# Attention and gated MLP on one core: V of the first two batches by casting transfers, one k sum moved into the matmuls, norms in two parts

## The chip, the core and the metric

The kernel runs on one core of a Trainium2 chip. The core has a matrix engine (TensorE, PE in the profile), a vector engine (VectorE, DVE), a scalar engine for functions and copies (ScalarE, ACT), a general engine that also issues transfers (GpSimd, POOL) and an engine that only issues transfers (SyncE, SP). Each runs its own stream of instructions in order; semaphores join them. [...]

The metric is the device time of one execution in microseconds (us), the median of ten runs. A transfer issued from GpSimd can convert float32 to bf16 on the way (a casting transfer); one issued from SP moves bytes as they are.

## The reference

Inputs are q, k and v of shape (8 batches, 8 heads, 576 positions, 64), and two weight matrices of 512 x 2048 and 2048 x 512, all float32. The output is float32, 4608 x 512.

```python
q_d = q.reshape(B, H, Sd, 4, D).mean(axis=3)      # k_d, v_d likewise; Sd = 144
out_d = softmax_attention(q_d, k_d, v_d)
out_up = np.repeat(out_d, 4, axis=2)
mask = np.abs(pos[:, None] - pos[None, :]) < 4
out_local = softmax_attention(q, k, v, where=mask)
x = (out_up + out_local) as (4608, 512)
h = x @ w_in
out = (h * sigmoid(1.702 * h)) @ w_out
```

So each batch has two attentions, a banded one at full length (each query sees at most seven keys) and a full one at a quarter of the length, over sums of four neighbours. Their sum goes through two matrix layers.

## The kernel before

The order of the instructions is written out by hand (`tc.manual_schedule`), so the order in the source is the order on each engine. Waits between engines are set by the framework from what each instruction reads and writes; for PSUM it takes a whole tile's bank as one thing.

**Groups.** The 4608 rows are taken in nine groups of 512 (`TG`). The loop over `g` (line 896) does, for group g, layer 1 (`mm1`, 16 chunks `ffc` of four matmuls, then a SiLU on ScalarE) and layer 2 (`mm2`, 64 matmuls, then a copy and a store), and meanwhile prepares and computes the attention of batch g + 1. The steps of that attention are functions, put into the stream of `mm1` and `mm2` at numbered slots: slots 0 to 15 are before the chunks of `mm1`, slot 16 + n is before matmul n of `mm2`. `POS` (line 778) has the seven slots for groups 1 and on, `POS_0` those for group 0, `VDP_0` the slot of a step that only batch 1 has.

**Batch 0's attention stands before the loop** (lines 787 to 890). Here TensorE has nothing else to do, and `warm` puts in matmuls of zeros that nobody reads; one float32 `warm` shows as two matmul rows of 0.5 us. The start ends in `part`, which does layer 1 of group 0 for the first six chunks as the head pairs' `xT` come in.

**Steps of one batch.** Heads are taken in two quads (`qd`) for scores and in four pairs (`hp`) after that.

- `prep_1` (275): VectorE turns a loaded k or q tile (32 x 32 blocks) into `kT` or `qT`, with positions along the free axis and two bf16 values (`a`) per position.
- `pool_qk` (298): GpSimd adds four neighbouring positions to `kdT` and `qdT`, two instructions each. `pool_q_reduce` (289) does it for q in one instruction on VectorE.
- `scores` (373): 80 matmuls of 60 columns into two PSUM tiles of `PA`, for five stretches of 114 positions. In batch 0 `bar_others` first writes a large negative number outside the band (`barred`). `scores_d` (395): 24 matmuls of 144 columns into one tile, for the short attention.
- `exp_local`, `exp_down` (412, 419): ScalarE, to `es` and `eds`.
- `av_local0` and `av_down0` (517, 531; batch 0), `av` (430; others): the products with V, with a column of ones that gives the sum of each row. V is in `vbs` (bf16, five chunks of 128 positions) and its sums of four in `vds`, which `prep_vd_pe` (337) makes in batches 0 and 1 by matmuls with a 0/1 matrix and a ScalarE copy.
- `normalise0` (547; batch 0) and `normalise` (475): VectorE, a reciprocal of the row sums and one or two multiplications to y.
- `transp_sum` and `copy_x` (called by `turned`, 869; batch 0), `transp`, `copy_od` and `merge` (others): TensorE turns y back, the result goes to `xT`, the input of layer 1.

PSUM has three tiles `PA[0..2]` of two banks and two tiles `PM[0..1]` of one. `ps_tile` hands out `PA` in turn, counted in `turn["a"]`; in batch 0 head pairs 0 and 1 take `PA[0]` and `PA[1]`, head pair 2 takes `PA[2]` after that, head pair 3 `PA[0]` again.

**Transfers.** `load_qk` (211), `load_w_in`, `load_w_out` and `load_vb` (231) are issued on GpSimd and cast. `load_v` (215) and `load_v4` are issued on SP in float32. V of batch 0 comes by `load_v` (ten transfers) and is cast by VectorE, a chunk at a time (`prep_v`). V of batch 1 comes by `load_v` for chunks 0 to 2, cast by GpSimd, and by `load_vb` for chunks 3 and 4. Some transfers are held back by a one-element copy (a gate) into their target, which has to wait for something else: line 795 for V of batch 0, line 812 for the layer-1 weights, lines 905 and 907 in group 0.

Of the kernel before, what the change touches and what calls it, by code (L numbers as in the profile page):

```python
# [8 lines left out]
FP32 = mybir.dt.float32  # L9
# [10 lines left out]
def kernel(  # L20
# [16 lines left out]
    n_ffc = d_ff // 128  # L37
    n_groups = B * S // TG
    inv_sqrt_d = 1.0 / math.sqrt(D)
    KSTART = (0, 56)  # L40
    QSTART = (0, 60)

# [24 lines left out]

    PA = [psum.tile([128, 2, 512], FP32, name=f"pa{i}") for i in range(3)]
    PM = [psum.tile([128, 512], FP32, name=f"pm{i}") for i in range(2)]
    turn = {"a": 0, "m": 0}  # L70

    def ps_tile(n=None):
        if n is None:
# [200 lines left out]

    def prep_1(name, b, qd):
        store, dst = {"k": (kf, kT), "q": (qf, qT)}[name]
        tt = work.tile([128, S, 2], BF16, name=f"{name}T{qd}", tag=f"{name}T{qd}", bufs=1)
        t32 = tt.rearrange("p t a -> p (t a)").bitcast(FP32)
        nc.vector.transpose(  # L279
            out=t32.rearrange("p (i c) -> p c i", c=18),  # L280
            in_=store[b, qd].bitcast(FP32).rearrange("p (c d) -> p c d", c=18),
        )
        dst[b, qd] = tt
# [14 lines left out]
    def pool_qk(b, qd, names="kq"):  # L298
        for name, src in (("k", kT), ("q", qT)):
            if name not in names:  # L300
                continue
            sv = src[b, qd].rearrange("p (j f) a -> p j f a", f=4)
            t1 = work.tile([128, SD, 2, 2], FP32, name="pq", tag="pq")
            nc.gpsimd.tensor_tensor(  # L304
                out=t1, in0=sv[:, :, 0:2, :], in1=sv[:, :, 2:4, :], op=ALU.add
            )
            if name == "k":
                dst = kdT[qd][:, 0:SD, :]
            else:
                t = work.tile([128, SD, 2], BF16, name=f"qdT{qd}", tag=f"qdT{qd}", bufs=1)  # L310
                qdT[b, qd] = t
                dst = t
            nc.gpsimd.tensor_tensor(
                out=dst, in0=t1[:, :, 0, :], in1=t1[:, :, 1, :], op=ALU.add
            )
# [54 lines left out]
                skip_group_check=True,  # L370
            )

    def scores(b, qd, barred=False):
        sp = [ps_tile(), ps_tile()]
        if barred:
            bar_others(sp)
        for i in range(5):
            for a in range(2):
                for par in range(2):
                    for r in range(4):  # L380
                        rows = slice(32 * r, 32 * r + 32)
                        k0 = 114 * i + KSTART[par]
                        q0 = 114 * i + QSTART[par]
                        nc.tensor.matmul(  # L384
                            sp[r // 2][64 * par : 64 * par + 64, r % 2, 60 * i : 60 * i + 60],
                            lhsT=kT[b, qd][rows, k0 : k0 + 64, a],
                            rhs=qT[b, qd][rows, q0 : q0 + 60, a],
                            start=(a == 0 and not barred),
                            stop=(a == 1 or barred),
                            tile_position=(32 * r, 64 * par),  # L390
                            skip_group_check=barred,
                        )
        return sp

    def scores_d(b, qd, sd=None):
        sd = sd or ps_tile()
        bank = banks(sd)
        for kc in range(3):
            for a in range(2):
                for r in range(4):  # L400
                    rows = slice(32 * r, 32 * r + 32)
                    j = r % 2
                    nc.tensor.matmul(  # L403
                        bank[r // 2][64 * j : 64 * j + 64, SD * kc : SD * kc + SD],
                        lhsT=kdT[qd][rows, 48 * kc : 48 * kc + 64, a],
                        rhs=qdT[b, qd][rows, :, a],
                        start=(a == 0), stop=(a == 1),
                        tile_position=(32 * r, 64 * j),
                    )
        return sd  # L410

    def exp_local(qd, sp):
# [131 lines left out]
                    tile_position=(64 * j, 64 * pos),  # L544
                )

    def normalise0(o):
        yl = work.tile([128, 2, 6, D], BF16, name="yl", tag="yl", bufs=4)
        yd = work.tile([128, 2, 2, D], BF16, name="yd", tag="yd", bufs=4)
        rc = work.tile([128, 2, 7, 1], FP32, name="rc", tag="rc")  # L550
        ov = o[:, :, 0:455].rearrange("p x (c e) -> p x c e", e=65)
        nc.vector.reciprocal(rc, ov[:, :, :, 64:65])
        nc.vector.tensor_tensor(
            out=yd.rearrange("p s x d -> p x s d"), in0=ov[:, :, 4:7:2, 0:D],
            in1=rc[:, :, 4:7:2].to_broadcast([128, 2, 2, D]), op=ALU.mult,
        )
        nc.vector.tensor_tensor(  # L557
            out=yl, in0=ov[:, :, 0:6, 0:D],
            in1=rc[:, :, 0:6].to_broadcast([128, 2, 6, D]), op=ALU.mult,
        )  # L560
        return yl, yd

    def transp_sum(y, x):
        y, yd = y
        ups = [
            (0, 6, sub(x[0], 3, (1, 228)), sub(up, 3, (228, 2), (1, 114))),
            (0, 6, sub(x[0], 0, (1, 3)), sub(up, 0, (1, 3))),
# [85 lines left out]
    def attention(b, slots=None):  # L653
# [18 lines left out]

        def avn(*hps):
            def f():
                for n, hp in enumerate(hps):
                    st["o", hp] = av(b, hp, slots and slots[n])
                for hp in hps:
                    st["y", hp] = normalise(st["o", hp])
            return f

        def tr(*hps):
            def f():
                for n, hp in enumerate(hps):
                    st["x", hp] = transp(st["y", hp], slots and slots[n])
                for hp in hps:
                    od = copy_od(st["x", hp])
                    merge(b, hp, st["x", hp], od)
            return f

        return [lambda: s_pe(0), lambda: s_act(0), s1, avn(0, 1), avn(2, 3), tr(0, 1), tr(2, 3)]  # L690

    def hps_mm(g, ffc, dmc, acc):
        nc.tensor.matmul(  # L693
# [82 lines left out]
            f()  # L776

    POS = [13, 16, 33, 42, 53, 62, 71]
    POS_0 = [16, 18, 27, 54, 68, 60, 76]
    VDP_0 = 52  # L780

    o, y, x = {}, {}, {}

# [8 lines left out]
    iota_psel()  # L792
    iota_up()
    fill()
    load_v(0, gate=after(kdT[1][0:1, SD, 0:1], nc.vector))
    warm(4)
    make_off()
    make_ident(di)
# [3 lines left out]
    make_up()  # L802
    prep_1("k", 0, 0)
    prep_1("q", 0, 0)
    pool_qk(0, 0)
    sp = scores(0, 0, barred=True)
    exp_local(0, sp)
    prep_1("k", 0, 1)
    prep_1("q", 0, 1)
    pool_q_reduce(0, 1)  # L810
    pool_qk(0, 1, "k")
    nc.gpsimd.tensor_copy(out=w_in_bf[0:1, 0, 0:1], in_=vf[0][0:1, 2, 0, 0:1])
    load_w_in(0, 512)
    load_w_in(512, 512)
    load_w_in(1024, 1024)
    for qd in range(NQ):
        load_qk(1, qd)
    load_w_out(0)
    load_w_out(1)
    for i in range(5):  # L820
        prep_v(0, nc.vector, i=slice(i, i + 1))
    warm(2)
    sd = scores_d(0, 0)
    exp_down(0, sd)
    sp = scores(0, 1, barred=True)
    exp_local(1, sp)
    for hp in range(2):
        o[hp] = PA[hp]
    warm(1)
    scores_d(0, 1, PM)  # L830
    for u in range(2):
        nc.scalar.activation(
            out=eds[1][:, u, 0:432], in_=PM[u][:, 0:432],
            func=AF.Exp, scale=inv_sqrt_d / 16.0,
        )
    nc.scalar.preload_act_table_set("silu_and_others")
    warm(1, t=PA[2][:, 0, :])
    for hp in range(2):
        av_local0(hp, o[hp], range(0, 3))
    warm(1, 384, PA[2][:, 0, :])  # L840
    for hp in range(2):
        av_local0(hp, o[hp], range(3, 4))
    prep_vd_pe(0, flat(PA[2]), range(0, 2))
    warm(1, 256)
    for hp in range(2):
        av_local0(hp, o[hp], range(4, 5))
    prep_vd_pe(0, pm_tile(), range(2, 3))
    warm(1, 256)
    for hp in range(2):
        av_down0(hp, o[hp])  # L850
        y[hp] = normalise0(o[hp])
    o[2] = PA[2]
    av_local0(2, PA[2], range(5))
    av_down0(2, PA[2])
    y[2] = normalise0(o[2])
    warm(1)
    warm(1, 256)
    make_mask()

    gT0 = new_gT()  # L860
# [11 lines left out]
        copy_x(0, hp, x)  # L872

    turned(0, None)
    o[3] = PA[0]
    av_local0(3, PA[0], range(5))
    av_down0(3, PA[0])
    y[3] = normalise0(PA[0])
    turned(1, 1)
    part((0, 1), 0)  # L880
    turned(2, 2)
# [7 lines left out]
    for ffc in range(6):  # L889
        silu(gT0, ffc, acc[ffc])  # L890

    def loads_2():
        load_v(2)
        load_v4(2)

    for g in range(n_groups):
        b = g + 1
        if g == 0:
            nc.gpsimd.memset(v4[32:64], 0.0)
            load_vb(1, 3)  # L900
            load_vb(1, 4)
            prep_qk(1, 0)
            pool_qk(1, 0)
            prep_qk(1, 1)
            load_v(1, gate=after(qf[1, 1][0:1, 0:1], nc.vector), chunks=range(3))
            pool_qk(1, 1)
            nc.gpsimd.tensor_copy(
                out=w_out_bf[0:1, 8, 0:1], in_=vf[1][0:1, 1, 0, 0:1]
            )
            load_w_out(2)  # L910
            load_w_out(3)
            for i in range(3):
                prep_v(1, nc.gpsimd, i=slice(i, i + 1))
            for qd in range(NQ):
                load_qk(2, qd)
            loads_2()
        elif b < B:
            if b > 2:
                load_v4(b)
# [50 lines left out]
```

## Time and profile before

| | |
|---|---|
| median of 10 runs | 329.1 us (327.51 to 333.52) |
| profiled execution, its own time | 329.75 us |
| its span, first to last instruction | 327.7 us |
| instructions in the span | 11050 |

Busy time of the engines by stage, from one table of windows (us; granted clock as a share of full speed; the DMA column is the mean busy share of the sixteen engines, over 1 where packets overlap):

| stage | PE | DVE | ACT | POOL | clock | DMA |
|---|---|---|---|---|---|---|
| 0 to 8.6: first loads, constants | 7.12 | 5.74 | 3.98 | 6.11 | 1.00 | 0.73 |
| 8.6 to 15.5: scores of batch 0 | 6.73 | 4.66 | 3.67 | 5.53 | 1.00 | 1.19 |
| 15.5 to 24.7: V products and norms of batch 0 | 9.14 | 5.06 | 4.63 | 7.44 | 1.00 | 1.15 |
| 24.7 to 40.4: layer 1 of group 0 | 15.23 | 7.59 | 10.29 | 10.01 | 1.00 | 1.30 |
| 40.4 to 66.1: layer 2 of group 0, attention of batch 1 | 21.30 | 12.43 | 12.99 | 5.84 | 1.00 | 1.08 |
| 66.1 to 327.7: the rest | 250.72 | 97.06 | 149.63 | 102.78 | 1.00 | 0.54 |

PE's busy time counts the fillers too, and a matmul's row is longer than the step to the next one: 128 x 512 bf16 matmuls have rows of 379 ns and follow each other every 216 ns.

In the views below, a row of a timeline has its start and length in us, the engine, the source line, the operation, the tiles it writes and reads, the shape, a count where equal rows are merged, and in brackets the idle time before it and what ended that.

### The profile page before, as it was taken

To read this page: it belongs to the slowest core of one execution; us is meant where nothing else is said; L and a number is where in the kernel's file an instruction comes from. 1 tells how busy PE (TensorE), PEld (TensorE's weight loads), DVE (VectorE), ACT (ScalarE), POOL (GpSimd) and SP (SyncE) were. 2 spreads that over 40 slices of the span, in tenths; PEclk is the share of its full clock that TensorE was granted. 3 is DMA by queue.
4 is the path that set the end of the run, shared out by engine and by line. 5 is a ranking of instruction groups with operands and counts; after the bars stand their busy time and mean duration, and the time that the engine had idled before them with its cause. 6 is when DMAs were issued, how large, how long until landed. Compare 5 with 4: busy or idle time off the path is not lost.

```text
span 327.7 us, 11050 instructions
## 1 busy us (share of the span) xinstructions
PE 310.2 (95%) x4908; PEld 159.0 (49%) x4962; DVE 132.5 (40%) x220; ACT 185.2 (57%) x322; POOL 137.7 (42%) x167
## 2 busy tenths in 40 slices
PE   8999979899999999999799999999999999999996
PEld 3564444445554555455444554455444544444444
DVE  6656342760676047703671277216730560000000
ACT  4645881566846582659166745775576646415611
POOL 7873861079406940596019901990098000000000
PEclk9999999999999999999999999999999999999999
DMA  7999999999817991699139942994180110011012
GB/s 123 185 196 210 183 134 196 191 234 222 151 68 156 206 155 36 159 198 191 39 103 181 191 110 72 198 191 126 50 160 3 66 38 32 0 68 62 0 54 75
DMA packets 63551, 41.08 MB, mean 125 GB/s; under 512 B 44048, under 2 KB 54416, under 8 KB 63504
## 3 DMA queue, kind: packets, MB, share of 16 engines
q1 hardware_dynamic: 52944, 26.42, 39.2%
q0 software_dynamic: 10416, 13.90, 24.9%
q8 instruction: 38, 0.62, 0.8%
q10 hardware_dynamic: 144, 0.07, 0.1%
q14 instruction: 9, 0.07, 0.1%
HBM read 44.83 MB, written 9.44 MB: 166 GB/s over the span
## 4 chain that ended last, share of the span: by engine, by line
PE 87%; DVE 5%; issue 4%; DMA 2%; ACT 1%; POOL 0%; ACTq 0%; DVEq 0%; POOLq 0%
PE pm L693 35%; PE pm L749 32%; PE pa L384 4%; PE pa L693 2%; PE pa L403 2%; PE pa L445 2%; DMA qb<-in_q_dram 2%; PE pa L467 2%; PE pa L749 2%; PE pa L498 2%; DVE xT L631 1%; PE pm L649 1%; PE pm L764 1%; DVE y L484 1%; DVE yl L557 1%
## 5 line engine op out<-in xcount | busy, mean ns | idle before, releaser
L693 PE MATMUL pm<-xT,w_in_bf 128*128 128x512 bf16 x528 | 120.3, 379 | 1.6 <-DVE xT L637 0.9
L749 PE MATMUL pm<-w_out_bf,gT 128*128 128x512 bf16 x493 | 114.1, 379 | 5.4 <-issue 5.2
L704 ACT ACTIVATE gT<-pm 128x512 bf16<-128x512 f32 x136 | 81.0, 598 | 46.1 <-PE pm L693 46.1
L693 PEld LDWEIGHTS <-w_in_bf 128*128 128x128 bf16 x576 | 55.6, 98 | 68.0 <-issue 1.9
L749 PEld LDWEIGHTS <-gT 128*128 128x128 bf16 x560 | 51.7, 98 | 59.5 <-issue 0.2
L304 POOL TENSOR_TENSOR pq<-kT 128x576 f32<-128x576 bf16 x16 | 18.5, 1158 | 98.1 <-DVE kT L279 98.1
L428 DVE TENSOR_TENSOR es<-es,mask 128x600 bf16<-128x600 bf16 x28 | 21.7, 791 | 90.8 <-ACT es L414 90.1
L734 ACT ACTIVATE osb<-pm 128x512 f32<-128x512 f32 (+2 forms) x35 | 20.8, 593 | 41.2 <-PE pm L749 37.3
L610 ACT COPY od<-pa 128x384 f32<-128x384 f32 (+1 forms) x56 | 18.4, 413 | 30.9 <-DVE y L484 18.7
L484 DVE TENSOR_TENSOR y<-pa,rc 128x896 bf16<-128x896 f32 x28 | 30.6, 1092 | 1.0
L631 DVE TENSOR_TENSOR xT<-pa,od 128x570 bf16<-128x570 f32 x28 | 21.1, 754 | 11.4 <-ACT od L610 11.0
L325 POOL TENSOR_TENSOR v<-v 112x512 f32<-112x512 f32 x18 | 22.8, 1265 | 0.0
L736 DVE TENSOR_SCALAR osb<-pm 128x128 f32<-128x128 f32 x1 | 0.3, 292 | 55.3 <-ACT osb L734 55.3
L414 ACT ACTIVATE es<-pa 128x600 bf16<-128x600 f32 x32 | 19.7, 668 | 2.8 <-PE pa L384 2.6
L279 DVE STREAM_TRANSPOSE kT<-kb 128x576 f32<-128x576 f32 x16 | 20.0, 1251 | 1.5 <-DMA kb<-in_k_dram 1.5
L279 DVE STREAM_TRANSPOSE qT<-qb 128x576 f32<-128x576 f32 x16 | 19.9, 1244 | 1.3 <-DMA qb<-in_q_dram 1.2
L304 POOL TENSOR_TENSOR pq<-qT 128x576 f32<-128x576 bf16 x15 | 17.2, 1146 | 0.0
L319 POOL CAST vb<-vf 128x2560 bf16<-128x2560 f32 (+1 forms) x9 | 16.1, 1809 | 0.0
L384 PEld LDWEIGHTS <-kT 32*64 32x64 bf16 x1280 | 12.0, 104 | 6.8 <-issue 5.6
L483 DVE RECIPROCAL rc<-pa 128x14 f32<-128x14 f32 x28 | 6.7, 241 | 20.7 <-PE pa L467 20.7
L420 ACT ACTIVATE ed<-pa 128x864 bf16<-128x864 f32 x15 | 13.5, 897 | 2.2 <-PE pa L403 2.2
L328 POOL TENSOR_TENSOR vd<-v 112x256 bf16<-112x256 f32 x18 | 13.7, 759 | 1.4
(104 smaller groups left out, 259.7 us busy)
## 6 DMA issues: line engine op xcount, KB each, us to landing
vf<-in_v_dram SPq DMA_DIRECT2D x76, 128.0 KB, 6.4
out_dram<-osb SPq DMA_DIRECT2D x35, 256.0 KB, 2.1
v<-in_v_dram SPq DMA_DIRECT2D x36, 192.0 KB, 5.8
kb<-in_k_dram POOLq DMA_DIRECT2D x16, 288.0 KB, 7.0
qb<-in_q_dram POOLq DMA_DIRECT2D x16, 288.0 KB, 9.3
w_out_bf<-in_moe_w_out_dram POOLq DMA_DIRECT2D x4, 512.0 KB, 8.3
w_in_bf<-in_moe_w_in_dram POOLq DMA_DIRECT2D x2, 512.0 KB, 8.5
w_in_bf<-in_moe_w_in_dram POOLq DMA_DIRECT2D x1, 1024.0 KB, 12.5
```

Of the source, the lines that this page charges most:

```text
L279: nc.vector.transpose(out=t32.rearrange("p (i c) -> p c i", c=18), in_=store[b, qd].bitcast(FP32).rearrange("p (c d) -> p c d", c=18),)
L304: nc.gpsimd.tensor_tensor(out=t1, in0=sv[:, :, 0:2, :], in1=sv[:, :, 2:4, :], op=ALU.add)
L325: eng.tensor_tensor(out=t1[0:112], in0=x[:, :, 0:2, :], in1=x[:, :, 2:4, :], op=ALU.add)
L384: nc.tensor.matmul(sp[r // 2][64 * par : 64 * par + 64, r % 2, 60 * i : 60 * i + 60], lhsT=kT[b, qd][rows, k0 : k0 + 64, a], rhs=qT[b, qd] ...
L414: nc.scalar.activation(out=es[2 * qd + u][:, :, 0:300], in_=sp[u][:, :, 0:300], func=AF.Exp, scale=inv_sqrt_d,)
L428: nc.vector.tensor_tensor(out=ev, in0=ev, in1=mask, op=ALU.mult)
L484: nc.vector.tensor_tensor(out=y[:, xs], in0=ov[:, :, :, 0:D], in1=rc[:, xs].to_broadcast([128, n, 7, D]), op=ALU.mult,)
L631: eng.tensor_tensor(out=sub(xT[hp], t0 + 3, (57, 2), (114, 5), (1, 57)), in0=sub(x, 3, (509, 2), (57, 5), (1, 57)), in1=sub(od, 3, (57, 2) ...
L693: nc.tensor.matmul(acc, lhsT=w_in_bf[:, dmc, ffc * 128 : (ffc + 1) * 128], rhs=xT[dmc][:, g * TG : g * TG + TG], start=(dmc == 0), stop=(d ...
L704: nc.scalar.activation(out=gT[:, ffc, :], in_=acc, func=AF.Silu, scale=GELU_SCALE)
L734: eng.activation(out=osb, in_=ap, func=AF.Copy, scale=1.0 / GELU_SCALE)
L749: nc.tensor.matmul(ops[t], lhsT=gT[:, ffc, t * 128 : (t + 1) * 128], rhs=w_out_bf[:, ffc, :], start=(ffc == 0), stop=(ffc == n_ffc - 1),)
```

## The change

V of batches 0 and 1 comes wholly by `load_vb`, ten casting transfers each, so the SP loads, the casts by VectorE and GpSimd and the four gates go. The loads of weights and of batch 1 move ahead of the constants' VectorE part in the source; on GpSimd they follow the ten V transfers at once. The sums of four of k for batch 0 are not made: `scores_d0` runs four matmuls, one for each of four neighbours, where `scores_d` ran one on the sum, reading `kT` with a step of four positions (`kT` gets a zeroed tail of 64 positions for that). q's sums of quad 0 move from GpSimd to VectorE. `normalise0` can be done in part "a" (slots 0 to 3) and part "b" (slots 4 to 6), and three head pairs now share the PSUM tiles at once, their "a" parts ahead of `prep_vd_pe` and of the last chunk. In batch 1, turning back is done one head pair at a time, in nine slots instead of seven. In group 0, GpSimd's issues of V stand between the sums of the two quads, and V of batch 2 waits on the last weights by a gate.

```diff
+    KP = S + 64
...
-    turn = {"a": 0, "m": 0}
+    turn = {"a": 2, "m": 0}
...
-        tt = work.tile([128, S, 2], BF16, name=f"{name}T{qd}", tag=f"{name}T{qd}", bufs=1)
-        t32 = tt.rearrange("p t a -> p (t a)").bitcast(FP32)
+        n = KP if name == "k" else S
+        tt = work.tile([128, n, 2], BF16, name=f"{name}T{qd}", tag=f"{name}T{qd}", bufs=1)
+        if b == 0 and n > S:
+            nc.vector.memset(tt[:, S:n, :], 0.0)
+        t32 = tt[:, 0:S, :].rearrange("p t a -> p (t a)").bitcast(FP32)
...
-    def scores(b, qd, barred=False):
-        sp = [ps_tile(), ps_tile()]
+    def scores(b, qd, barred=False, sp=None):
+        sp = sp or [ps_tile(), ps_tile()]
...
+    def scores_d0(qd, sd):
+        bank = banks(sd)
+        for kc in range(3):
+            for a in range(2):
+                for f in range(4):
+                    for r in range(4):
+                        rows = slice(32 * r, 32 * r + 32)
+                        j = r % 2
+                        k0 = 192 * kc + f
+                        nc.tensor.matmul(
+                            bank[r // 2][64 * j : 64 * j + 64, SD * kc : SD * kc + SD],
+                            lhsT=kT[0, qd][rows, k0 : k0 + 253 : 4, a],
+                            rhs=qdT[0, qd][rows, :, a],
+                            start=(a == 0 and f == 0), stop=(a == 1 and f == 3),
+                            tile_position=(32 * r, 64 * j),
+                        )
...
+    def normalise0(o, y, parts="ab"):
+        yl, yd, rc = y
         ov = o[:, :, 0:455].rearrange("p x (c e) -> p x c e", e=65)
-        nc.vector.reciprocal(rc, ov[:, :, :, 64:65])
+        c0, c1 = {"a": (0, 4), "b": (4, 7), "ab": (0, 7)}[parts]
+        nc.vector.reciprocal(rc[:, :, c0:c1], ov[:, :, c0:c1, 64:65])
+        if "b" in parts:
+            nc.vector.tensor_tensor(
+                out=yd.rearrange("p s x d -> p x s d"), in0=ov[:, :, 4:7:2, 0:D],
+                in1=rc[:, :, 4:7:2].to_broadcast([128, 2, 2, D]), op=ALU.mult,
+            )
+            c1 = 6
         nc.vector.tensor_tensor(
-            out=yd.rearrange("p s x d -> p x s d"), in0=ov[:, :, 4:7:2, 0:D],
-            in1=rc[:, :, 4:7:2].to_broadcast([128, 2, 2, D]), op=ALU.mult,
-        )
-        nc.vector.tensor_tensor(
-            out=yl, in0=ov[:, :, 0:6, 0:D],
-            in1=rc[:, :, 0:6].to_broadcast([128, 2, 6, D]), op=ALU.mult,
-        )
-        return yl, yd
+            out=yl[:, :, c0:c1], in0=ov[:, :, c0:c1, 0:D],
+            in1=rc[:, :, c0:c1].to_broadcast([128, 2, c1 - c0, D]), op=ALU.mult,
+        )
...
         def tr(*hps):
             def f():
...
+                for hp in hps:
+                    st["x", hp] = transp(st["y", hp], slots and slots[hp % 2])
...
                     od = copy_od(st["x", hp])
                     merge(b, hp, st["x", hp], od)
             return f
 
-        return [lambda: s_pe(0), lambda: s_act(0), s1, avn(0, 1), avn(2, 3), tr(0, 1), tr(2, 3)]
+        first = [lambda: s_pe(0), lambda: s_act(0), s1, avn(0, 1)]
+        if b == 1:
+            return first + [tr(0), tr(1), avn(2, 3), tr(2), tr(3)]
+        return first + [avn(2, 3), tr(0, 1), tr(2, 3)]
...
-    POS_0 = [16, 18, 27, 54, 68, 60, 76]
-    VDP_0 = 52
+    POS_0 = [16, 18, 27, 48, 52, 57, 66, 70, 75]
+    VDP_0 = 44
...
-    load_v(0, gate=after(kdT[1][0:1, SD, 0:1], nc.vector))
+    for i in range(5):
+        load_vb(0, i)
+    load_w_in(0, 512)
+    load_w_in(512, 512)
+    load_w_in(1024, 1024)
+    for qd in range(NQ):
+        load_qk(1, qd)
+    load_w_out(0)
+    load_w_out(1)
...
-    pool_qk(0, 0)
-    sp = scores(0, 0, barred=True)
+    sp = scores(0, 0, barred=True, sp=PA[0:2])
     exp_local(0, sp)
     prep_1("k", 0, 1)
+    pool_q_reduce(0, 0)
     prep_1("q", 0, 1)
     pool_q_reduce(0, 1)
-    pool_qk(0, 1, "k")
-    nc.gpsimd.tensor_copy(out=w_in_bf[0:1, 0, 0:1], in_=vf[0][0:1, 2, 0, 0:1])
-    load_w_in(0, 512)
...
     warm(2)
-    sd = scores_d(0, 0)
-    exp_down(0, sd)
-    sp = scores(0, 1, barred=True)
+    exp_down(0, scores_d0(0, PA[2]))
+    sp = scores(0, 1, barred=True, sp=PA[0:2])
     exp_local(1, sp)
-    for hp in range(2):
-        o[hp] = PA[hp]
-    warm(1)
-    scores_d(0, 1, PM)
+    scores_d0(1, PM)
...
+    for hp in range(4):
+        o[hp] = PA[hp % 3]
+        y[hp] = y_tiles0()
+    for i in (range(3), range(3, 4)):
+        for hp in range(3):
+            av_local0(hp, o[hp], i)
+    for hp in range(3):
+        normalise0(o[hp], y[hp], "a")
+    prep_vd_pe(0, PM[0], range(0, 2))
+    prep_vd_pe(0, PM[1], range(2, 3))
     nc.scalar.preload_act_table_set("silu_and_others")
-    warm(1, t=PA[2][:, 0, :])
-    for hp in range(2):
-        av_local0(hp, o[hp], range(0, 3))
-    warm(1, 384, PA[2][:, 0, :])
-    for hp in range(2):
-        av_local0(hp, o[hp], range(3, 4))
-    prep_vd_pe(0, flat(PA[2]), range(0, 2))
-    warm(1, 256)
-    for hp in range(2):
+    for hp in range(3):
         av_local0(hp, o[hp], range(4, 5))
-    prep_vd_pe(0, pm_tile(), range(2, 3))
-    warm(1, 256)
-    for hp in range(2):
+        if hp == 0:
+            warm(1, 256, PM[0])
         av_down0(hp, o[hp])
-        y[hp] = normalise0(o[hp])
-    o[2] = PA[2]
-    av_local0(2, PA[2], range(5))
-    av_down0(2, PA[2])
-    y[2] = normalise0(o[2])
-    warm(1)
-    warm(1, 256)
+        normalise0(o[hp], y[hp], "b")
+    warm(1, t=PM[0])
...
-    o[3] = PA[0]
-    av_local0(3, PA[0], range(5))
-    av_down0(3, PA[0])
-    y[3] = normalise0(PA[0])
+    av_local0(3, o[3], range(5))
+    av_down0(3, o[3])
+    normalise0(o[3], y[3])
...
+            load_vb(1, 0)
+            load_vb(1, 1)
+            prep_qk(1, 0)
+            pool_qk(1, 0)
+            load_vb(1, 2)
+            prep_qk(1, 1)
+            pool_qk(1, 1)
             load_vb(1, 3)
             load_vb(1, 4)
-            prep_qk(1, 0)
-            pool_qk(1, 0)
-            prep_qk(1, 1)
-            load_v(1, gate=after(qf[1, 1][0:1, 0:1], nc.vector), chunks=range(3))
-            pool_qk(1, 1)
-            nc.gpsimd.tensor_copy(
-                out=w_out_bf[0:1, 8, 0:1], in_=vf[1][0:1, 1, 0, 0:1]
-            )
             load_w_out(2)
             load_w_out(3)
-            for i in range(3):
-                prep_v(1, nc.gpsimd, i=slice(i, i + 1))
             for qd in range(NQ):
                 load_qk(2, qd)
-            loads_2()
+            load_v(2, gate=after(w_out_bf[0:1, 12, 0:1], nc.gpsimd))
+            load_v4(2)
```

More of the change, by code (lines that the diff above doesn't have):

```diff
@@ L301, in pool_qk @@
                 continue
-            sv = src[b, qd].rearrange("p (j f) a -> p j f a", f=4)
+            sv = src[b, qd][:, 0:S, :].rearrange("p (j f) a -> p j f a", f=4)
             t1 = work.tile([128, SD, 2, 2], FP32, name="pq", tag="pq")
@@ L409, in scores_d @@
                     )
+        return sd
+    def scores_d0(qd, sd):
[14 more added lines that the diff above has]
+                        )
         return sd
@@ L545, in av_down0, with y_tiles0 @@
                 )
[L547 to L550, printed above, removed]
-        ov = o[:, :, 0:455].rearrange("p x (c e) -> p x c e", e=65)
-        nc.vector.reciprocal(rc, ov[:, :, :, 64:65])
+    def y_tiles0():
+        return (
+            work.tile([128, 2, 6, D], BF16, name="yl", tag="yl", bufs=4),
+            work.tile([128, 2, 2, D], BF16, name="yd", tag="yd", bufs=4),
+            work.tile([128, 2, 7, 1], FP32, name="rc0", tag="rc0", bufs=4),
+        )
+    def normalise0(o, y, parts="ab"):
+        yl, yd, rc = y
+        ov = o[:, :, 0:455].rearrange("p x (c e) -> p x c e", e=65)
+        c0, c1 = {"a": (0, 4), "b": (4, 7), "ab": (0, 7)}[parts]
[6 more added lines that the diff above has]
+            c1 = 6
         nc.vector.tensor_tensor(
-            out=yd.rearrange("p s x d -> p x s d"), in0=ov[:, :, 4:7:2, 0:D],
-            in1=rc[:, :, 4:7:2].to_broadcast([128, 2, 2, D]), op=ALU.mult,
-        )
-        nc.vector.tensor_tensor(
-            out=yl, in0=ov[:, :, 0:6, 0:D],
-            in1=rc[:, :, 0:6].to_broadcast([128, 2, 6, D]), op=ALU.mult,
-        )
-        return yl, yd
+            out=yl[:, :, c0:c1], in0=ov[:, :, c0:c1, 0:D],
+            in1=rc[:, :, c0:c1].to_broadcast([128, 2, c1 - c0, D]), op=ALU.mult,
+        )
     def transp_sum(y, x):
-        y, yd = y
+        y, yd = y[:2]
         ups = [
@@ L674, in f @@
             def f():
-                for n, hp in enumerate(hps):
-                    st["o", hp] = av(b, hp, slots and slots[n])
+                for hp in hps:
+                    st["o", hp] = av(b, hp, slots and slots[hp % 2])
                 for hp in hps:
@@ L682, in f @@
             def f():
-                for n, hp in enumerate(hps):
-                    st["x", hp] = transp(st["y", hp], slots and slots[n])
+                for hp in hps:
+                    st["x", hp] = transp(st["y", hp], slots and slots[hp % 2])
                 for hp in hps:
@@ L804 @@
     prep_1("q", 0, 0)
-    pool_qk(0, 0)
-    sp = scores(0, 0, barred=True)
+    sp = scores(0, 0, barred=True, sp=PA[0:2])
     exp_local(0, sp)
     prep_1("k", 0, 1)
+    pool_q_reduce(0, 0)
     prep_1("q", 0, 1)
     pool_q_reduce(0, 1)
-    pool_qk(0, 1, "k")
-    nc.gpsimd.tensor_copy(out=w_in_bf[0:1, 0, 0:1], in_=vf[0][0:1, 2, 0, 0:1])
-    load_w_in(0, 512)
[L814 to L821, printed above, removed]
     warm(2)
-    sd = scores_d(0, 0)
-    exp_down(0, sd)
-    sp = scores(0, 1, barred=True)
+    exp_down(0, scores_d0(0, PA[2]))
+    sp = scores(0, 1, barred=True, sp=PA[0:2])
     exp_local(1, sp)
-    for hp in range(2):
-        o[hp] = PA[hp]
-    warm(1)
-    scores_d(0, 1, PM)
+    scores_d0(1, PM)
     for u in range(2):
@@ L890 @@
         silu(gT0, ffc, acc[ffc])
-    def loads_2():
-        load_v(2)
-        load_v4(2)
     for g in range(n_groups):
```

## The prediction

> **What bounds the kernel now.** I read the strips of the page first, then the chain of waits, then TensorE's timeline where the chain says "issue", then the DMA queues there.
>
> ```profile
> PE   8999979899999999999799999999999999999996
> ...
> PEclk9999999999999999999999999999999999999999
> DMA  7999999999817991699139942994180110011012
> ```
>
> TensorE (PE) is busy in nearly every slice at the full granted clock; from 4 to 44 us the DMA engines are full too. So a saving counts only where PE waits or runs filler: before the first layer-1 matmul (24.7 us, with `warm` fillers), and in group 0's layer 2 (40.4 to 66.1 us). Later batches keep their code. The chain of waits at the end of the start:
>
> ```profile
> 20.98 0.26 DVE rc L552
> ...
> 21.60 0.95 DVE yl L557
> 22.55 0.16 DVE rc L552
> ...
> 24.64 0.88 DVE yl L557
> 25.51 0.04 issue
> 25.55 0.47 PE pa L573 x5
> ```
>
> Columns: start, length, what. VectorE's norms, 1.48 us per head pair (20.98, 22.47, 23.94), set y2 = 25.5; from there PE runs without a gap, `turned(3)` at 27.09 to 27.83. In group 0, PE waits 0.73 us for y (57.61) and 0.22 + 0.50 us for xT (65.26, 66.14), and shows waits of another kind:
>
> ```profile
> 14.50 0.97 PE L403 MATMUL pm<-qdT,kdT 32*64 32x144 bf16 x24
> 44.03 0.84 PE L384 MATMUL pa<-qT,kT 32*64 32x60 bf16 x80
> 46.53 0.58 PE L403 MATMUL pa<-qdT,kdT 32*64 32x144 bf16 x24 [1.67 <-ACT es L414]
> 157.53 0.34 PE L467 MATMUL pa<-vd,ed 48*64 48x65 bf16 x15 [1.42 <-issue]
> ```
>
> At 46.53 the line blames an exp that `scores_d` doesn't need; at 157.53 it names nobody. Counting PE's weight loads and matmuls from the start (a `warm` leaves four: 13 warms 52, bars 16, scores 320, scores_d 96, av 320, vd 28, transp_sum 120, mm1 128; batch 1's scores 320, scores_d 48; eleven mm2 22) gives 1470 at 46.5. The trace has breaks also at 1979 (60.75), 4015 (122.01), 5288 (157.53), and a small one at 449 (15.16, why line one takes 0.97 us for what takes 0.58 elsewhere): multiples of 254.5 recorded instructions. At each, a packet of the instruction queue had just ended:
>
> ```profile
> q8 instruction: 38, 0.62, 0.8%
> ```
>
> 38 packets of 16 KB, 256 instructions each. Packets ended 1.60, 1.62, 1.46, 1.49, 1.42 us before PE went on at those breaks. **So PE's program comes in blocks of 256**: entering one starts the fetch of the next, and dense small matmuls (160 instructions in 0.64 us) eat a block before the next is there.
>
> [...] Entry to readiness of the next block, where PE enters late and the entry is thus known: 15.1 to 21.0 (packet 17.93, 1.58 long, +1.5), 21.05 to 27.3 (packet 24.78), 46.43 to 52.9, all with DMA full; 122.01 to 125.9 and 157.53 to 161.1 with DMA slack. So **6.0 us with DMA full, 3.6 to 3.9 with slack**.
>
> **The start, without blocks.**
> - *V by casting.* Removed: five VectorE casts and their waits (13.34 to 18.2), 16 of SP's V issues, four gate copies (two each on Pool and VectorE) and Pool's three casts of batch 1. Added: ten Pool issues (and six more for batch 1) at 0.68 us (the row of line 233). Pool goes from `iota_up` (end 6.3) to 13.1 on them, against w_in's first issue at 14.44: w_in, k/q 1 and w_out 0,1 come some 1.2 us earlier. Packets: 512 of 128 B per DMA. [...]
> - *k sums on PE.* Removed: Pool's sums (three pairs, 7.38 to 13.0). Added: 96 instead of 24 matmuls per quad, at 0.51 us per 24: 2.04, so +1.53 twice; and one q sum on VectorE, 1.35 us, between k01 and q01, so q01 is turned at 12.6 instead of 12.04, covered by PE being in `scores_d0` till 13.65. The tail memsets (0.1 us) hide in the wait for q except about 0.04. The weights now have a step of 16 B instead of 4; no row has that. Below: 0. Above: weights of 64 columns take twice their share, +0.05 us per four, 2.4 us. Nearest row is line 403 itself: 0, both ends kept.
> - *PE order*, ends: scores 9.6, warm(2) 11.6, scores_d0 13.65, scores 15.15, scores_d0 17.2, av chunks 0 to 3 of three head pairs 17.95. ScalarE's exps end at 18.3, its vd copies at 19.8; the table load and mask behind them end at 21.8, before the first xT copy is wanted (22.8).
> - *Norms in parts.* "a": reciprocal 0.27 + 512 elements 0.60 = 0.87; "b": 0.27 + 0.34 + 0.34 = 0.95. VectorE is free by then, and chunk 4 of a head pair waits on PE for its "a" (same tile), with the down matmuls behind it; b would queue behind the third "a" anyway. a from 18.0 to 20.6, b to 21.6, 22.5, 23.5; y3 at 24.95 against 26.98. `turned(3)`, with the parts before it on PE, begins at 26.0 against 27.1 to 27.26: **−1.25**, with 0.9 us to spare ahead of "a".
>
> **The start, with blocks.** Instructions: scores_d0 +288, five warms fewer −20: +268, about one block more in the same stage. Boundaries at 195, 451, 707, 963, 1219. In the new order scores end at 184, warm 192, scores_d0 384, scores 552, scores_d0 744, av chunks 840, vd 868, hp0 920, hp1 968, hp2 1016.
> - 451 falls in `scores(0,1)`, wanted at 14.5; the block lands at 15.1 now, with less traffic on the engines then: about 14.5. No stall.
> - 707 falls in the second `scores_d0`, wanted at 16.8. 14.5 + 6.0 = 20.5 (18.1 by the short time). PE stands 3.7 us.
> - 963 falls at the end of hp1's av_down0: 20.5 + 6.2 = 26.7 (21.7). "a" parts and b of hp0 are done in this wait.
> - From there: hp2 0.3, warm 1.05, turned(0) 0.74, av 3 0.58, turned(1) 0.7, part 0.43, turned(2) 0.72, parts 0.86 = 5.4: `turned(3)` at 32.1. Against 27.2: **+4.9**. With short times VectorE limits: y2 24.8, turned(3) 27.0, −0.3.
> DMA is full in this stage (V, then w_in's 2 KB reads), so I take the full row.
>
> **Group 0.** Head pair by head pair, y has four matmuls more to hide (tr(0) four slots after av: y0 at +1.85, wanted at +1.95), xT one slot more. The 0.73, 0.22 and 0.50 go, and the 0.41 at 60.34, whose block boundary (1987) now meets a longer stretch; two more insertions at 0.16 to 0.2 come: **−1.5** (ends −1.9 and +0.5). The 1.77 at `scores_d(1,1)` stays: 268 is a block and 12, so boundary 1731 lies before it again (1738). V of batch 1 has to be in at slot 44 instead of 52: Pool issues it between its pair sums, last at about 46, landed at 49; slot 44 comes at 54. Five us of cover. Pool's queue behind: w_out 2, 3 issue at 46 to 47.7, landing 52 and 54.6; wanted at 56 and later; k/q 2 behind them, 53 to 59, as now. V of batch 2, gated by a Pool copy on w_out 3 (behind it on Pool are only the sums of 67 us), starts at 54.6 instead of 52.4; wanted at 73. Behind it on SP stand the stores of group 0, now issued at 66.89; 2 us later costs nothing, as four output buffers hold them and group 1 writes its first after 80. Later groups: same code, 0 ± 1 for shifted boundaries.
>
> **Sum.** +4.9 − 1.5 = +3.4. The profiled execution took 329.75 with a span of 327.7, 0.65 over the median; the difference is added to the median: 329.1 + 3.4 = **332.5**; its own range 330 to 335.5.
>
> **Rivals.**
> - *Blocks don't bind* (blocks in 3.6 us, since Pool paces V's packets and leaves gaps, or fetched further ahead): −1.25 to −0.3, − 1.5: 326.4 to 327.3, faster. For: at 122 us it was 3.9. Against: every start block took about 6. It decides where the blocks for 707 and 963 together take under 7.8 us from 14.5 (turned(3) by 27.7) instead of 12.2.
> - *Half-way*: blocks in about 4.4 us; turned(3) at 28.7; +1.5 − 1.5: 329.1.
> - *Strided weights alone*: 2.4 us on PE less 0.9 to spare: +0.25 − 1.5: 327.9. For: nothing in the trace has this step.
> - *The clock falls*: PE would stand twice for over 3 us. The trace has no such stand (1.77 us is the longest) and no lower clock to price it by. At half clock for some 3 us after it, +1.5 to 3: 334 to 335.5.
> - *V late at slot 44*: from 5 us of delay on; too far.
>
> **Chances.** Forecast 0.55 (0.03 of it within 0.3%), clock 0.10, half-way 0.10 (0.02 slower, 0.06 same, 0.02 faster), blocks don't bind 0.17, strided 0.08 (0.01 same). Over 0.3% (1.0 us, what a measurement can tell): slower 0.64, same 0.10, faster 0.26. Range 326.8 to 336: it leaves about 0.1 below and less above.
>
> **What would show it.** Breaks of PE near recorded instructions 707 (in the second run of `scores_d0`) and 963, each 1.5 us after a q8 packet; `turned(3)` near 32. Wrong: `scores_d0` in 2.0 us both times and turned(3) by 27; or matmuls of `scores_d0` evenly slower. In group 0, no wait of line 498 for y.

## The result and the profile after

The changed kernel takes 331.7 us (median of 14 executions, 329.3 to 332.8) against 328.7 for the kernel before (51 executions): the ratio is 1.0082, with an interval of 1.0058 to 1.0106; it leaves out a few slow executions of the kernel before, which the medians have in them. The profiled spans stand at 330.6 and 327.7 us. So it is slower by 2.7 us (ratio) to 3.0 us (medians); the forecast was +3.4. The sum came out nearly right by luck: its terms were off in opposite directions.

The rows of the page that answer to those of before:

```profile
PE   6958999999999999999899999999999999999996
...
DVE  6516602690378127712573077306740570000000
...
PEclk9987999999999999999999999999999999999999
DMA  7999959999943992299319951995190110011012
...
q8 instruction: 40, 0.66, 0.8%
```

PE now has a hole in the third slice (16.5 to 24.8 us). DVE is nearly idle there (1), so it isn't VectorE that holds it up. The granted clock, full throughout before, is below full in the third and fourth slices. There are two instruction packets more than the 38 of before.

TensorE's timeline through that hole (start, length, engine, line, operation, how many; in brackets the idle time before it and what ended it):

```profile
11.33 3.11 PE L425 MATMUL pa<-qdT,kT 32*64 32x144 bf16 x96 [0.27 <-DVE qdT L297]
14.37 0.68 PE L369 MATMUL pa<-off,id 128*128 128x300 bf16 x4
14.98 0.84 PE L388 MATMUL pa<-qT,kT 32*64 32x60 bf16 x80
15.62 2.50 PE L425 MATMUL pm<-qdT,kT 32*64 32x144 bf16 x75
21.84 0.88 PE L425 MATMUL pm<-qdT,kT 32*64 32x144 bf16 x21 [3.71 <-issue]
...
27.76 0.22 PE L561 MATMUL pa<-vd,ed 48*64 48x65 bf16 x2 [1.02 <-issue]
...
28.16 1.96 PE L678 MATMUL pm<-wz 128*128 128x512 f32 x2
...
34.45 0.47 PE L602 MATMUL pa<-up,yd 128*128 128x228 bf16 x5
```

The last row is `turned(3)`, the fourth head pair's turning back. In the kernel before it was

```profile
27.09 0.47 PE L573 MATMUL pa<-up,yd 128*128 128x228 bf16 x5
```

PE stands 3.71 us in the middle of the second `scores_d0` and names nobody ("issue"). Counted from the start, the first instruction after it is recorded number 705 and the one at 27.76 is 961, 256 further on; the forecast put the breaks at 707 and 963. From 16 to 22 us the instruction queue moved one packet,

```profile
q8 instruction: 1, 0.02, 1.0%
```

from 19.59 to 20.53. The next ended at 26.48. PE went on 1.31 and 1.28 us after these ends. From 34.45 against 27.09, the start is **7.4 us longer** (forecast: 4.9).

Two more things stand in these rows. Ninety-six matmuls of `scores_d0` take 3.11 us, where the forecast had 2.04. And the `warm` pair at 28.16 takes 1.96 us against 1.1 elsewhere. The table of windows says why (window, busy time of PE, PEld, DVE, ACT and POOL, granted clock, DMA share, GB/s):

```profile
17.85:21.84 3.99, 0.28 (x12) 0.14 (x7) 0.00 (x0) 0.00 (x0) 1.87 (x3) 0.96 1.22 206
21.84:25.00 3.16, 3.16 (x83) 2.65 (x82) 1.26 (x4) 1.04 (x3) 2.65 (x2) 0.51 1.12 212
25.00:28.30 3.30, 2.08 (x79) 1.39 (x76) 2.41 (x8) 2.74 (x4) 0.26 (x1) 1.00 1.12 212
28.30:31.70 3.40, 3.40 (x57) 1.82 (x57) 1.60 (x5) 0.57 (x2) 1.78 (x3) 0.50 1.12 210
```

The clock is at half for 3.41 us twice, from 21.50 and from 28.32; the two stands, of 3.71 and 1.02 us, end at 21.84 and 27.76. The DMA engines are full all along (share over 1), at over 200 GB/s.

In group 0 (`scores(1,0)` to `scores(2,0)`) the changed kernel takes 33.5 us (47.8 to 81.3) where before took 36.4 (40.4 to 76.8): **2.9 us won** (forecast: 1.5). Of the other traces with the new group 0 (the experiments below), five took 33.1 to 33.6 us there, and two lost time to a load or a block and took 35.8 and 36.5; the second trace with the old group 0 took 35.9. The waits of the changed kernel there:

```profile
52.48 0.23 PE L388 MATMUL pa<-qT,kT 32*64 32x60 bf16 x6 [0.30 <-issue]
...
60.85 0.35 PE L520 MATMUL pa<-id,y 60*64 60x60 bf16 x20 [0.22 <-DVE y L506]
```

The wait for y has shrunk from 0.73 to 0.22 us, and the one for xT is gone. The break that the forecast let stand (recorded 1470 of before; 1.77 us as the forecast counts it, 1.67 by its row) is the first row, now number 1726, and takes 0.30.

Behind group 0 another 1.6 us is won. Before had block breaks of 0.43 us at 122.0 and 1.42 at 157.5; after has one of 0.81, at 160.75, which makes 1.0 of it; what makes the rest is open. The sum by the two traces: 7.4 − 2.9 − 1.6 = +2.9.

### The profile page after: what moved, and what is told of

The parts are those of the page before. It is cut to its first block, busy times and chain, and to the rows that moved or that the text cites. A ratio compares the mean times of both kernels' runs of the same rounds, so it can differ in the third digit from the quotient of the medians.

```text
span 330.6 us, 11290 instructions
## 1 busy us (share of the span) xinstructions
PE 311.6 (94%) x5042; PEld 163.0 (49%) x5096; DVE 130.1 (39%) x222; ACT 185.1 (56%) x322; POOL 140.8 (43%) x173
## 4 chain that ended last, share of the span: by engine, by line
PE 91%; issue 4%; DMA 2%; DVE 2%; POOL 0%; ACT 0%; DVEq 0%; POOLq 0%
PE pm L725 35%; PE pm L781 34%; PE pa L388 4%; PE pa L725 2%; PE pa L781 2%; PE pa L520 2%; DMA kb<-in_k_dram 2%; PE pa L467 2%; PE pa L407 2%; PE pa L489 1%; PE pm L796 1%; PE pm L425 1%; PE pa L425 1%; PE pm L678 1%; DVE y L506 1%
## 5 line engine op out<-in xcount | busy, mean ns | idle before, releaser
L308 POOL TENSOR_TENSOR pq<-kT 128x576 f32<-128x576 bf16 x14 | 16.2, 1157 | 96.2 <-DVE kT L283 96.2
L450 DVE TENSOR_TENSOR es<-es,mask 128x600 bf16<-128x600 bf16 x28 | 20.1, 733 | 93.3 <-ACT es L436 92.5
L308 POOL TENSOR_TENSOR pq<-qT 128x576 f32<-128x576 bf16 x14 | 16.0, 1146 | 0.0
L234 POOL DMA_DIRECT2D vb<-in_v_dram x20 | 13.7, 702 | 5.0 <-DMA w_in_bf<-in_moe_w_in_dram 3.5
L388 PE MATMUL pa<-qT,kT 32*64 32x60 bf16 x1280 | 14.1, 203 | 1.5 <-DVE kT L281 1.2
```

What stands on the lines that cost most here:

```text
L308: nc.gpsimd.tensor_tensor(out=t1, in0=sv[:, :, 0:2, :], in1=sv[:, :, 2:4, :], op=ALU.add)
L388: nc.tensor.matmul(sp[r // 2][64 * par : 64 * par + 64, r % 2, 60 * i : 60 * i + 60], lhsT=kT[b, qd][rows, k0 : k0 + 64, a], rhs=qT[b, qd] ...
L450: nc.vector.tensor_tensor(out=ev, in0=ev, in1=mask, op=ALU.mult)
```

## The experiments

**The k sums on VectorE.** The changed kernel, but with k of batch 0 summed by two VectorE reductions, so that the short scores are 24 matmuls again.

```diff
+    pool_k_reduce(0, 0)
...
-    exp_down(0, scores_d0(0, PA[2]))
     sp = scores(0, 1, barred=True, sp=PA[0:2])
     exp_local(1, sp)
-    scores_d0(1, PM)
+    warm(1)
+    exp_down(0, scores_d(0, 0, PA[2]))
+    warm(2)
+    scores_d(0, 1, PM)
```

The short scores of quad 0 move behind the scores of quad 1 with this, and three `warm` are added.

> k of batch 0 is summed by VectorE (two instructions of about 1.35 us) and scores_d runs 24 matmuls per quad again; all else as in the changed kernel. Blocks theory: 288 instructions fewer in the start, so no stand of PE over 0.7 us between 9 and 24 us apart from waits for data; the block for recorded instruction 707 is met only in the down products of head pair 2, about 22 us; turned(3) begins at 26 to 27.2 (34.45 now), and with group 0's gain kept the kernel takes 325.5 to 327.5, faster than before. Strided weights alone as the cause: turned(3) comes 2.1 us earlier than now, about 32, and the time stays above the kernel before.

327.6 us, ratio 0.9941 (0.9923 to 0.9959): with this one part undone, the rest wins. But `turned(3)` came at 30.24 and not at 26 to 27.2, so the expectation for the start was missed, and with it, narrowly, that for the time. Its timeline has the block break again, later in the program:

```profile
22.37 0.55 PE L569 MATMUL pa<-vd,ed 48*64 48x65 bf16 x19 [1.87 <-issue]
```

It is number 705 again. Fewer instructions moved it to the third head pair, and its packet still started late (19.98). The clock was at half from 22.1 to 28.9 us.

**Weights in a row.** The same number of matmuls, with weights from 64 neighbouring positions (a step of 4 bytes instead of 16, since two bf16 values are kept per position). The kernel computes other sums.

```diff
-                            lhsT=kT[0, qd][rows, k0 : k0 + 253 : 4, a],
+                            lhsT=kT[0, qd][rows, k0 : k0 + 64, a],
```

> scores_d0 takes 64 neighbouring positions as weights instead of every fourth (other sums are computed, the same number of instructions). Strided weights cost: the first scores_d0 takes 2.05 us instead of 3.11. Blocks theory: the break at recorded instruction 705 stays and gets longer, since PE is there a us earlier (4 us or more, going on at 20.5 to 21.8), and turned(3) is at 33 to 34.5, at most 1 us earlier than now. If strided weights were the cause: no break over 1 us and turned(3) at 30 or earlier.

```profile
10.99 1.74 PE L425 MATMUL pa<-qdT,kT 32*64 32x144 bf16 x96
14.07 0.61 PE L388 MATMUL pa<-qT,kT 32*64 32x60 bf16 x53 [0.48 <-issue]
14.48 1.42 PE L425 MATMUL pm<-qdT,kT 32*64 32x144 bf16 x75
20.81 0.87 PE L425 MATMUL pm<-qdT,kT 32*64 32x144 bf16 x21 [4.92 <-issue]
```

The longer step costs 3.11 − 1.74 = 1.37 us per 96 matmuls. More than half of what its absence wins is hidden under the block here: PE is at the break 2.2 us sooner (15.9 against 18.1), and the break is 1.2 us longer, ending 1.0 sooner. `turned(3)` came 2.5 us sooner than in the changed kernel, at 31.93, and sooner than expected. The other 1.5 us are the clock: from the second break to `turned(3)`, the same instructions, this kernel took 5.20 us (26.73 to 31.93, clock 0.99) and the changed one 6.69 (27.76 to 34.45, half speed for 3.4 of them). The kernel took 329.4 us, in one execution.

**Fifty-six instructions ahead.** Small `warm` matmuls, before the first scores, shift everything behind them.

```diff
-    warm(4)
+    warm(3)
+    warm(15, 16)
```

> One warm of 512 columns is replaced by fifteen of 16 columns in the first idle time, 56 PE instructions more ahead of the scores. Blocks theory: the long break stays at recorded instruction 705 and so moves 56 instructions up in the code: after about 47 of the 96 matmuls of the second scores_d0 instead of 75; the next, at 961, moves from head pair 1's down products into head pair 0's. A wait for data (a semaphore, PSUM, a transfer) would keep both at the same matmul: after 75, and in head pair 1.

```profile
16.57 1.66 PE L425 MATMUL pm<-qdT,kT 32*64 32x144 bf16 x47
21.83 1.72 PE L425 MATMUL pm<-qdT,kT 32*64 32x144 bf16 x49 [3.60 <-issue]
...
33.67 0.18 PE L613 MATMUL pa<-id,yl 60*128 60x60 bf16 x1 [2.38 <-issue]
```

The break now stands after 47 matmuls of `scores_d0` instead of 75, which is 28 matmuls and their 28 weight loads sooner: exactly 56. It is still number 705, so it belongs to the count and not to anything that those matmuls read. The next, 961, stands in head pair 0's down products, as expected (27.75, after 0.64 us). A third boundary (1217, again 256 further on) came to lie ahead of `turned(3)` and cost another 2.38 us: 336.8 us in all, in one execution.

**The DMA engines kept free.** A GpSimd copy that reads the last `es` holds back the loads of w_in, k/q 1 and w_out.

```diff
+    nc.gpsimd.tensor_copy(out=w_in_bf[0:1, 0, 0:1], in_=es[3][0:1, 0, 0:1])
+    load_w_in(0, 512)
...
+    load_w_out(1)
```

> The weights of layer 1, and the loads behind them on GpSimd, wait by a gate for the second exp_local (about 17 us) instead of following V at once. Blocks delayed by full DMA engines: the block that PE enters about 15 us starts by 17.2 instead of 19.59, the break at 705 ends by 19.8 instead of 21.84 and is 1.5 to 2 us shorter; turned(3) at 32 to 33, unless layer 1 then waits for its weights. If the fetch is slow whatever else moves: it starts at 19 or later and the break stays.

```profile
15.29 2.51 PE L425 MATMUL pm<-qdT,kT 32*64 32x144 bf16 x75
18.63 0.83 PE L425 MATMUL pm<-qdT,kT 32*64 32x144 bf16 x21 [0.84 <-issue]
...
25.10 0.22 PE L561 MATMUL pa<-vd,ed 48*64 48x65 bf16 x2 [2.39 <-issue]
```

The packet started at 16.29 instead of 19.59 and the first break shrank from 3.71 to 0.84 us. The block after it, entered at 18.6 with the held loads now running, took 6.5 us, and the break at 961 grew to 2.39. So a block's time was longer with the loads ahead of its fetch: 3.9 us from entry to going on (14.77 to 18.63) without them, 6.5 with them, in one execution. `turned(3)` came at 31.78, 2.7 us sooner than in the changed kernel. 328.2 us, ratio 0.9972 (0.9951 to 0.9993).

**Both together.** k sums on VectorE, and the loads held back (here on the first `eds`).

> As the version with k summed by VectorE, and the weights of layer 1 wait by a gate on GpSimd for exp_down of quad 0 (about 15.5 us), so that they leave the DMA engines to the instruction block that PE enters at about 16.4. Blocks theory: that packet starts by 18 (19.98 without the gate), the break of 1.87 us in head pair 2's down products shrinks below 0.5, TensorE's clock does not fall after it, turned(3) begins at 27 to 28.5 (30.24 without), time 324.5 to 327, at least 1 us under the version without the gate. If the gate only moves the loads: turned(3) unchanged, or layer 1 waits for its weights and the time rises.

```profile
25.55 0.47 PE L610 MATMUL pa<-up,yd 128*128 128x228 bf16 x5
```

There is no block break before this `turned(3)`, which came sooner than expected and 1.5 us sooner than before. 325.5 us, ratio 0.9908 (0.9881 to 0.9935). It lost 1.4 us of that again in group 0, to a late load of w_out:

```profile
53.23 1.02 PE L789 MATMUL pm<-w_out_bf,gT 128*128 128x512 bf16 x3 [1.35 <-DMA w_out_bf<-in_moe_w_out_dram]
```

**The group-0 part alone.** The start of before with the change's batch 1: V by casting transfers, its place at slot 44, and the transposes head pair by head pair.

```diff
-    POS_0 = [16, 18, 27, 54, 68, 60, 76]
-    VDP_0 = 52
+    POS_0 = [16, 18, 27, 48, 52, 57, 66, 70, 75]
+    VDP_0 = 44
...
+            load_vb(1, 0)
...
-            load_v(1, gate=after(qf[1, 1][0:1, 0:1], nc.vector), chunks=range(3))
```

> The kernel before with the change's group 0 only: V of batch 1 by casting transfers, the nine slots, turning head pair by head pair; the start as before. Part alone is worth 1.5 us or more: turned(3) stays at 27.1, waits for y and xT in layer 2 of group 0 go, scores of batch 2 come at 74 to 75.5 (76.80 before), 326 to 327.8, ratio 0.991 to 0.997. If the 2.85 us that group 0 got back in the changed kernel were only slack after a late start: scores of batch 2 at 76 or later, ratio 0.998 or more.

**324.6 us, ratio 0.987 (0.9825 to 0.9914)**: the lowest of all, faster than both kernels and than expected (its interval overlaps that of "both together"). Its `turned(3)` of the start (26.8) is nearly as before. Group 0 takes 33.1 us (40.1 to 73.2; 74 at the soonest was expected) against 36.4, and the short scores follow the scores with no stand:

```profile
44.46 0.58 PE L403 MATMUL pa<-qdT,kdT 32*64 32x144 bf16 x24
...
52.71 0.35 PE L498 MATMUL pa<-id,y 60*64 60x60 bf16 x20 [0.21 <-DVE y L484]
```

Number 1470 stands there, where before lost 1.67 us. Between entering that block and its packet (40.6 to 41.5) the engines moved 51 GB/s; in the kernel before, 186 (40.9 to 43.4). Their busy share was no lower, 1.58 against 1.40.

**The k sums on TensorE alone.** The start of before with `scores_d0`, and none of the other parts.

```diff
-    sd = scores_d(0, 0)
+    sd = scores_d0(0, ps_tile())
...
-    scores_d(0, 1, PM)
+    scores_d0(1, PM)
```

> The kernel before with the k sums of batch 0 on PE only (scores_d0 with every fourth position as weights); V, norms and group 0 as before. Blocks theory: a break of 2 to 4 us at recorded instruction 705, in the second scores_d0; turned(3) 3 to 7 us later than the 27.1 before; 331 to 335, ratio 1.007 to 1.02. If what costs is strided weights alone: no break over 1 us, turned(3) within 2.5 us of before.

```profile
11.28 3.10 PE L425 MATMUL pa<-qdT,kT 32*64 32x144 bf16 x96
16.75 3.10 PE L425 MATMUL pm<-qdT,kT 32*64 32x144 bf16 x96
...
51.21 0.27 PE L388 MATMUL pa<-qT,kT 32*64 32x60 bf16 x16 [1.31 <-issue]
```

333.6 us, ratio 1.0142 (1.0066 to 1.0218). The break expected at 705 did not come: the packet started at 16.40, 1.4 us after PE entered the block ahead of it, and PE reached the boundary at 18.9. `turned(3)` came at 32.27, 5.2 us late, which is also more than the 2.5 that the expectation gives to strided weights alone. It is what the matmuls themselves cost: 2 x (3.10 − 0.51), with the clock full. So `scores_d0` costs some 5 us with no break at all: 2.5 by the number of matmuls (2 x 1.23, at the 1.74 us of the weights in a row) and 2.7 by the step of the weights (2 x 1.37). In the changed kernel part of that lies under breaks that would have been there for fewer or faster instructions too. With the old transfers of batch 1 the break in group 0 is there (last row).

**w_out earlier.** The kernel of "both together", with w_out 2 issued ahead of the third load of V.

```diff
+            load_w_out(2)
             load_vb(1, 2)
...
-            load_w_out(2)
             load_w_out(3)
```

> The kernel of e5_dve_sums_w_in_held, with the load of w_out 2 put ahead of the third load of V of batch 1 instead of behind the fifth. In e5 PE stood 1.42 us at 51.81, in group 0's layer 2, for a w_out load issued at 46.57 that took 7.6 us to land; the same load was issued at 44.09 in e6. If that wait is all that e5 lost there, it goes and nothing takes its place: scores(2,0) at 73.2 instead of 74.62, time 324.1 (ratio about 0.986), level with e6. Rival: the loads share full DMA engines then (V of batch 1 and k/q 2 come later by what w_out 2 takes, some 2.5 us), so that the third V load is late at the vd step of batch 1, or another block of instructions is: time as in e5, 325.5, or over.

The second case of the expectation came true. The wait for w_out went, and in its place came

```profile
43.69 0.25 PE L415 MATMUL pa<-qdT,kdT 32*64 32x144 bf16 x3 [0.77 <-POOL qdT L325]
46.04 0.55 PE L415 MATMUL pa<-qdT,kdT 32*64 32x144 bf16 x21 [2.10 <-issue]
```

a block break of 2.10 us, number 1470 once more, its packet starting at 43.24 instead of 41.45. `scores(2,0)` came at 74.93. 327.0 us, ratio 0.9945 (0.9913 to 0.9977), whose interval overlaps that of "both together".

## Why the forecast came out as it did

**What bounds the start: right.** The breaks came two recorded instructions from where they were counted, each 1.3 us after a packet. They moved with the count (56 instructions, 28 matmuls), shrank when the DMA engines were freed (3.71 to 0.84), and went when both instructions and traffic were taken away. The rival that blocks don't bind falls. The causes don't add up one by one, since each covers another: from 34.45 us, `turned(3)` came 4.2 sooner without the k sums in the matmuls, 2.5 without the longer step, 2.7 with the loads held back, and 8.9 with the first and the third together.

**The size of the start: 4.9 forecast, 7.4 measured.** Three terms were off; the blocks (+1.1) and the clock (+1.3) make up the difference.

- *"I take the full row"*: 6.0 us per block. The block entered at 15.10, not 14.5, and took 6.7 us; the next took 5.9. Together the break at 961 ended 1.06 us later than the 26.7 of the forecast. w_in's first issue, brought forward from 14.44 to 13.15 by the change itself, is part of this: held back, the same block took 3.9 us.
- *"0, both ends kept", for the step of the weights*: it is 1.37 us per 96 matmuls. The forecast took the row of the operation with the short step and kept 2.4 us as its upper end; two times 1.37 passes that. It did not show in the forecast's sum because most of it lay under the first break: PE reached it at 18.1 and not 16.8, and the 3.71 us it then stood agree with the forecast's 3.7 by luck: the block was as late as PE was.
- *The clock*, set apart as a rival of 0.10. It fell too. From 27.76 to `turned(3)` 6.69 us against 5.4 forecast (+1.3). The comparison above puts 1.5 us on a stretch of 3.4 us at half speed. Executions of one kernel agree with that: with the DMA engines kept free, ten at a mean clock of about 0.995 (one such stretch) took 328.6 on average, eight at full clock 327.1. No execution of the changed kernel was above 0.995. In the changed kernel it was no alternative to the breaks but followed them, and belonged in the forecast.

**Norms in parts, V by casting: −1.25 forecast, not measured.** That sum had 96 matmuls per quad and no blocks. The 1.5 us of "both together" were won with no blocks, but with 24. In the changed kernel VectorE waits 9.9 us for PE (to 23.67), and from the break at 27.76 to `turned(3)` PE has no wait for VectorE over 0.15 us, so finishing the norms sooner could win nothing there.

**Group 0: −1.5 forecast, −2.9 measured.** The waits for y and xT went as worked out. *"The 1.77 at `scores_d(1,1)` stays"* failed: the count was right (the boundary does lie there), but the block's time was taken as given. In the changed kernel it took 4.3 us (48.2 to 52.5) against 5.6 (40.9 to 46.5). The likely cause is that batch 1's V no longer came as float32 at that moment: the engines moved 90 GB/s from entry to fetch (48.2 to 49.6) instead of 186, though their busy share was much the same (1.30 against 1.40). In seven of the eight traces with the new group 0 the packet started 0.9 to 2.0 us after entry (4.2 in "w_out earlier"), in the two with the old one after 2.5 and 2.9. A run with only V's transfers changed was not made, so this stays likely and not shown.

**Later groups: 0 ± 1 forecast, −1.6 measured**, 1.0 of it by the block breaks.

**V late at slot 44** didn't happen: no wait for it shows in group 0.

## What to carry to other kernels

Moving a sum from another engine into TensorE's matmuls costs instructions (here 288 more weight loads and matmuls for the two sums) even where the time seems free: count them, find the block boundaries of the program in the trace, and ask which loads stand in front of each fetch. A load that is brought forward can delay the program itself: here a packet of instructions started at 19.59 us with the loads at once and at 16.29 with them held back. And where a forecast has TensorE stand for several microseconds, a half-speed stretch behind it (here 3.41 us long, 1.5 us lost in it) is to be weighed as a term of the sum.

## What the hardware showed beside

- **Weights with a step.** With weights of 64 columns at a step of 16 bytes, 32-row, 144-column matmuls in a dense run followed each other every 32 ns, at a step of 4 bytes every 18 ns (3.11 and 1.74 us for 96). No run tried other steps.
- **Half speed came in lengths of 3.41 us.** Apart from the end of the kernel, the stretches at half speed in these traces lasted 3.41 us or twice that (changed kernel 3.41 twice, DMA kept free 3.4, k sums on VectorE and weights in a row 6.8 each). In the 3.41 us ahead of each, PE was busy for 0 to 64% (changed kernel 1% and 64%, k sums on VectorE 49%, DMA kept free 30%, 56 instructions ahead 0%); a fall followed stands of 1.87 and 2.39 us as well as 3.71. But none followed the 1.67 us of the kernel before (PE busy for 47% from 44.89 to 48.30), nor the 2.10 of "w_out earlier" (17% in the 3.44 us up to 46.04). So no limit can be read off.
- **The time of a fetch went with the loads issued ahead of it, and varied.** The packet of the block from recorded instruction 705 on started 3.4 to 4.5 us after PE got to number 449, where the block ahead of it begins, in the four traces with w_in's loads issued at 13.1 us (changed kernel 15.10 to 19.59), and 0.2 to 1.5 in the three with them held back. With the start of before it was 2.8, 1.2 and 1.4 us (before 15.16 to 17.93, group-0 part alone 14.88 to 16.03, k sums on TensorE alone 15.04 to 16.40). The rate alone doesn't tell: the engines moved 143 GB/s in the first of these three stretches and 169 in the second.
